# Decode of w_in in a PSUM bank, and the next chunk's transposes between the two halves of the second layer

## The chip, the cores and the metric

One core of a Trainium2 chip runs the kernel as one program. It has five engines with instruction queues of their own: TensorE (PE in the profile; its weight loads are PEld), VectorE (DVE), ScalarE (ACT), GpSimd (POOL) and SyncE (SP), which here only issues DMAs. The metric is the device time of one execution in microseconds (us).

## The reference

Attention, then a mixture of experts with a skip gate, then a two-layer net; everything in float32:

```
x   = attention(q, k, v)                  # block-causal, 4 x 8 heads, 576 tokens, head 64 -> x is 2304 x 512
do  = x @ w_skip > 0;  e = argmax(x @ w_gate)                # 8 experts
x[do] += gate * (relu(x @ w1[e]) @ w2[e])                    # w1: 512 x 1024, w2: 1024 x 512 per expert
h   = x @ w_in                                               # w_in: 512 x 2048
out = (max(h, 0) + alpha * min(h, 0)) @ w_out                # w_out: 2048 x 512
```

`w_in` and `w_out` come in as 64-bit floats, two 32-bit words per number, `hw` and `lw`; the kernel turns them into a float32 and splits that into two parts `hi` and `lo` for the matmuls. This turning is the "decode".

## The kernel before, in words

Three stages follow each other: attention (0 to about 265 us of the span), the experts (about 265 to 472 us) and the two-layer net (the rest). The change lies in the expert stage.

**Chunks of an expert.** For each expert `e` the list of its tokens is known. The first 32 go through a small path that packs tokens of four experts (`s_one`, `s_ht`, `s_two`). If there are more than 32 (a branch on the register `areg[e]`, in `extra`), the rest goes in chunks of 128 tokens. A chunk is gathered from the DRAM tensor `xd` by an indirect DMA that GpSimd issues (`gather`, line 579), transposed on TensorE through PSUM (`xt`, which calls `trans`, line 677; ScalarE copies the result to `xT`), goes through the first layer (`full1`, line 742: 32 matmuls, two ps_h tiles, ScalarE relu), and the second (`full2`, line 751: 8 matmuls of 512 columns, accumulated in one ps_y tile). ScalarE scales the result (line 753), GpSimd adds the old rows (line 754) and scatters the sum back to `xd` (line 582). The trace records each of these float32 matmuls twice, so full1 shows as x64 and full2 as x16. A last chunk of at most 64 tokens goes through `half` (lines 765 and 773).

`chunk` sets the order. On GpSimd the gather of the next chunk is issued before this chunk's add and scatter, so it stands behind the chunk before this one's add and scatter. On TensorE the next chunk's transposes stand between full1 and full2:

```
            if nxt:
                nxt.gather()
            ch.full1()
            if nxt:
                nxt.xt()
            ch.full2()
```

The first chunk of expert e+2 is gathered ahead (`level0`, after expert e is done). Where an expert has at most 32 tokens, its branch is skipped, and GpSimd then waits at the end of the skipped part until all its earlier DMAs have landed.

**Decode on VectorE.** w_in is 16 pieces of 128 x 512, decoded in the expert stage by `dec_in` (`decode` with `alone` and `halves`): ten VectorE operations (lines 628 to 636, 615 and 619) on each of two halves of 256 columns, with a scratch tile `dt` in SBUF for each half. `DEC` says how many pieces stand at which expert: none before and one behind the loads for expert 0's iteration, then 2 and 1, 2 and 2, 2 and 3, 3 and 0. The pieces of w_out and their decode (128 x 512 in one part, `w_dec`) come at the end of the stage (the first two, in `first_decode`) and in the first part of the last stage.

**Loads on SP.** All large loads stand in one queue, in program order, and a load waits until the one two places ahead has landed (`bulk`, DEPTH 2). A decode of piece m is followed by the load of piece m+3 (`dec_load`), which has to wait until VectorE has read piece m, since there are three raw tiles `dr`. Behind the loads of pieces 16, 17 and 18 (the first of w_out) stand the eight loads of expert 7's weights (`load_w(7)`), which also need that expert 4 is done with its buffers. Behind those, in `first_window`, stand the four loads of `xz`, the first 512 rows of x for the last stage; these wait for every gather and scatter before them. `first_window` also issues `s_two(7)` and the transposes of xz and the rows of the small path into four PSUM tiles `px` (lines 885 and 888), with which the last stage starts.

PSUM in the expert stage is eight banks: ps_t 2, ps_h 4, ps_y 2.

Of the kernel before, what the change touches and what calls it, by code (L numbers as in the profile page):

```python
# [9 lines left out]
F32 = mybir.dt.float32  # L10
# [7 lines left out]
PSUM = bass.MemoryType.PSUM  # L18
# [29 lines left out]
def tile_kernel(ctx: ExitStack, tc: tile.TileContext, q, k, v, w_skip, w_gate, w1, w2, w_in, w_out, alpha, out):  # L48
# [18 lines left out]
    wide = w_in.dtype != F32  # L67
# [529 lines left out]
    wpool["b2"] = mp("wb", 1)  # L597
    mw = mp("mw", 2)
    ps_t = mp("ps_t", 2, space=PSUM)
    ps_h = mp("ps_h", 4, space=PSUM)  # L600
    ps_y = mp("ps_y", 2, space=PSUM)

    def decode(n, hi, lo, tmp, alone, halves):
        wsp[n] = hi, lo
        a = raw.pop(n)
        V, P = nc.vector, nc.gpsimd
        parts = 2 if halves else 1
        n1 = 512 // parts
        cs = [slice(i * n1, i * n1 + n1) for i in range(parts)]
        ts = [tmp() if wide else a[:, c] for c in cs]  # L610

        def split():
            for t, c in zip(ts, cs):
                if halves:
                    V.tensor_copy(out=hi[:, c], in_=t)
                else:
                    nc.scalar.activation(out=hi[:, c], in_=t, func=AF.Copy)
            for t, c in zip(ts, cs):
                V.tensor_tensor(out=lo[:, c], in0=t, in1=hi[:, c].bitcast(F32), op=ALU.subtract)

        def each(fn):
            for t, c in zip(ts, cs):
                fn(t, t.bitcast(I32), a[:, c, 1], a[:, c, 0])

        if wide:
            if not alone:
                each(lambda t, ti, hw, lw: nc.scalar.activation(out=lw.bitcast(F32), in_=lw.bitcast(U32), func=AF.Copy, scale=2.0 ** -52))
            each(lambda t, ti, hw, lw: V.tensor_scalar(out=ti, in0=hw, scalar1=0x7FFFFFFF, scalar2=None, op0=ALU.bitwise_and))  # L628
            each(lambda t, ti, hw, lw: V.tensor_scalar(out=hw, in0=hw, scalar1=-2 ** 31, scalar2=None, op0=ALU.bitwise_and))
            each(lambda t, ti, hw, lw: V.tensor_scalar(out=t, in0=t, scalar1=_f32(TINY), scalar2=_f32(HUGE), op0=ALU.max, op1=ALU.min))  # L630
            each(lambda t, ti, hw, lw: V.tensor_scalar(out=ti, in0=ti, scalar1=4, scalar2=-2 ** 31, op0=ALU.logical_shift_left, op1=ALU.bitwise_xor))
            each(lambda t, ti, hw, lw: V.scalar_tensor_tensor(out=ti, in0=ti, scalar=1, in1=hw, op0=ALU.logical_shift_right, op1=ALU.bitwise_or))
            each(lambda t, ti, hw, lw: V.tensor_scalar(out=hw, in0=ti, scalar1=-2 ** 23, scalar2=None, op0=ALU.bitwise_and))
            if alone:
                each(lambda t, ti, hw, lw: V.scalar_tensor_tensor(out=lw.bitcast(F32), in0=lw.bitcast(U32), scalar=2.0 ** -52, in1=hw.bitcast(F32), op0=ALU.mult, op1=ALU.mult))
                each(lambda t, ti, hw, lw: V.tensor_tensor(out=t, in0=t, in1=lw.bitcast(F32), op=ALU.add))
            else:
                each(lambda t, ti, hw, lw: P.tensor_tensor(out=lw.bitcast(F32), in0=lw.bitcast(F32), in1=hw.bitcast(F32), op=ALU.mult))
                each(lambda t, ti, hw, lw: P.tensor_tensor(out=t, in0=t, in1=lw.bitcast(F32), op=ALU.add))
        if halves:  # L640
            split()
        return split
# [3 lines left out]
    def dec_in(n):  # L646
        for i in range(n):
            m = next(decs, None)
            if m is None:
                return  # L650
            hi = wip.tile([128, 512], F32R, tag="hi", name="whi")
            lo = wip.tile([128, 512], F32R, tag="lo", name="wlo")
            decode(m, hi, lo, lambda: mw.tile([128, 256], F32, tag="dt", name="dt"), True, True)
            if m + 3 < 19:
                dec_load(m + 3)

# [66 lines left out]
    class Chunk:  # L723
# [20 lines left out]
                nc.scalar.activation(out=h, in_=ps, func=AF.Relu)  # L744
                self.hT.append(h)

        def full2(self):
            w = wt[self.e][1]
            ps = ps_y.tile([128, 512], F32, tag="y", name="psy")
            for kk in range(8):  # L750
                nc.tensor.matmul(ps, self.hT[kk // 4][:, kk % 4], w[:, kk], start=(kk == 0), stop=(kk == 7))  # L751
            yo = mw.tile([128, DM], F32, tag="yo", name="yo")
            nc.scalar.activation(out=yo, in_=ps, func=AF.Copy, scale=self.gate)
            nc.gpsimd.tensor_tensor(out=yo, in0=yo, in1=self.xg, op=ALU.add)
            scatter(yo, self.ids)
# [33 lines left out]
    def chunk(e, ch, i, xg, xT):  # L789
        off = 32 + 128 * i  # L790
        nxt = Chunk(e, li[i + 1][:, e], xg[i % 2], xT[(i + 1) % 2]) if i + 1 < KX else None
        with tc.If(areg[e] > off + 64) as many:
            if nxt:
                nxt.gather()
            ch.full1()
            if nxt:
                nxt.xt()
            ch.full2()
            with tc.If(areg[e] > off + 128):
                if nxt:  # L800
                    chunk(e, nxt, i + 1, xg, xT)
                else:
                    with tc.For_i(off + 128, areg[e], 128) as r:
                        l = mw.tile([128, 2], I32, tag="ll", name="ll", bufs=1)
                        nc.gpsimd.dma_start(out=l, in_=lv[e, bass.ds(r, 128), :])
                        more = Chunk(e, l, xg[0], xT[0])
                        more.gather()
                        more.xt()
                        more.full1()
                        more.full2()  # L810
        with many.Else():
            ch.half()
# [4 lines left out]
    nxt = {}  # L817
# [56 lines left out]
    def first_window():  # L874
        xz = xzs[0]
        for t in range(4):
            nc.sync.dma_start(out=xz[:, t], in_=xd[t * 128:t * 128 + 128, :])
        for f in range(EARLY):
            dec_load(16 + f + 3)
        s_two(E - 1)  # L880
        new_x(0)
        px = [ps_h.tile([128, 4, 128], F32, tag="h", name="psx") for t in range(4)]
        for t in range(4):
            for kk in range(4):
                nc.tensor.matmul(px[t][:, kk], xz[:, t, kk * 128:kk * 128 + 128], ident, start=(kk == 0), stop=False, is_transpose=True, skip_group_check=True)
        for t in range(4):
            for kk in range(4):
                nc.tensor.matmul(px[t][:, kk], sy[1][:, kk * 128:kk * 128 + 128], xz[:, 5, t * 128:t * 128 + 128], start=False, stop=True, skip_group_check=True)
            split_x(0, t, px[t])
        for f in range(EARLY):  # L890
            w_split(f)
        for f in range(EARLY, 3):
            w_dec(f, lambda: xz[:, (6, 7, 4)[f]])
# [160 lines left out]
```

## Time and profile before

| what | value |
|---|---|
| three runs | 896.58, 897.37, 899.27 us; median 897.37 |
| profiled execution, its own time | 903.32 us |
| its span, first to last instruction | 901.7 us |
| TensorE busy | 818.0 us (91%) |
| VectorE busy | 440.4 us (49%) |
| GpSimd busy | 218.5 us (24%) |
| granted TensorE clock, mean | 0.952 of full speed |

The span is told in us from its start. The profiled execution took 0.66% longer than the median run; differences that are worked out in the span are taken off both. Busy shares are means over stages that differ: in the last stage (575 to 901.7 us) TensorE works 322.50 of 326.70 us, in the expert stage it waits in several places.

### The profile page before, as it was taken

To read this page: it belongs to the slowest core of one execution; us is meant where nothing else is said; L and a number is where in the kernel's file an instruction comes from. 1 tells how busy PE (TensorE), PEld (TensorE's weight loads), DVE (VectorE), ACT (ScalarE), POOL (GpSimd) and SP (SyncE) were. 2 spreads that over 40 slices of the span, in tenths; PEclk is the share of its full clock that TensorE was granted. 3 is DMA by queue.
4 is the path that set the end of the run, shared out by engine and by line. 5 is a ranking of instruction groups with operands and counts; after the bars stand their busy time and mean duration, and the time that the engine had idled before them with its cause. 6 is when DMAs were issued, how large, how long until landed. Compare 5 with 4: busy or idle time off the path is not lost.

```text
span 901.7 us, 15294 instructions
## 1 busy us (share of the span) xinstructions
PE 818.0 (91%) x5804; PEld 629.7 (70%) x5804; DVE 440.4 (49%) x1091; ACT 303.3 (34%) x793; POOL 218.5 (24%) x225
## 2 busy tenths in 40 slices
PE   7999999999975578857869988799999999999998
PEld 4777777777754454645547766588888888888897
DVE  4466757566646077654047999522332233223232
ACT  3666676766642121201225344321112111211121
POOL 1000110100126132243313654422222222222221
PEclk7999999999998698978979999899999999999999
DMA  6665354454215877762452222110011000100000
GB/s 132 150 181 138 79 140 104 113 128 134 74 51 123 260 249 246 227 221 84 141 188 91 79 74 67 47 47 1 0 48 47 1 1 23 47 1 1 23 26 24
DMA packets 96381, 85.87 MB, mean 95 GB/s; under 512 B 68601, under 2 KB 73913, under 8 KB 96272
## 3 DMA queue, kind: packets, MB, share of 16 engines
q1 hardware_dynamic: 93776, 78.88, 30.0%
q0 software_dynamic: 2496, 5.61, 2.2%
q8 instruction: 60, 0.98, 0.5%
q14 instruction: 49, 0.40, 0.1%
HBM read 73.20 MB, written 11.71 MB: 94 GB/s over the span
## 4 chain that ended last, share of the span: by engine, by line
PE 64%; DVE 11%; DMA 9%; issue 9%; POOL 3%; ACT 1%; another core or an unknown queue 1%; SPq 1%; POOLq 0%; DVEq 0%; ACTq 0%
PE psf L955 18%; PE psa L988 6%; PE psa L987 6%; PE pso L315 6%; PE psa L997 5%; PE pspt L296 5%; PE pss L236 5%; DMA xgs<-xd,sid 4%; PE psy L751 2%; PE pss L242 2%; PE pso L308 2%; DVE gt L966 2%; DVE mx L249 1%; DMA w1t<-in_moe_w_dram 1%; DVE dt L628 1%
## 5 line engine op out<-in xcount | busy, mean ns | idle before, releaser
L955 PE MATMUL psf<-xs,whi 128*128 128x512 f32 (+1 forms) x640 | 161.5, 375 | 6.1 <-ACT xs L843 6.1
L973 POOL TENSOR_TENSOR gl<-gt,gh 128x512 fp32r<-128x512 f32 (+1 forms) x72 | 85.3, 1185 | 250.4 <-PE psa L997 137.0
L955 PEld LDWEIGHTS psf<-xs,whi 128*128 128x128 f32 x640 | 115.5, 190 | 31.5 <-ACT xs L843 6.7
L972 ACT ACTIVATE gh<-gt 128x512 fp32r<-128x512 f32 (+1 forms) x80 | 47.1, 589 | 256.9 <-PE psa L988 149.7
L968 DVE TENSOR_SCALAR gu<-psf,alf 128x512 f32<-128x512 f32 (+1 forms) x64 | 43.7, 683 | 167.1 <-PE psf L955 166.9
L955 PE MATMUL psf<-xs,wlo 128*128 128x512 f32 (+1 forms) x320 | 81.0, 375 | 0.0
L266 ACT ACTIVATE pe<-pss,mx 128x512 f32<-128x512 f32 (+3 forms) x128 | 66.4, 522 | 12.0 <-DVE mx L249 10.1
L249 DVE TENSOR_REDUCE mx<-pss 128x2 f32<-128x1024 f32 (+1 forms) x64 | 52.5, 820 | 32.2 <-PE pss L238 29.3
L955 PEld LDWEIGHTS psf<-xs,wlo 128*128 128x128 f32 x320 | 57.2, 190 | 11.8
L274 ACT ACTIVATE pt<-pspt 128x512 f32<-128x512 f32 (+3 forms) x112 | 52.0, 487 | 34.9 <-PE pspt L296 33.5
L987 PE MATMUL psa<-whi,gh 128*128 128x512 f32 x144 | 57.6, 400 | 4.0 <-ACT gh L972 4.0
L315 PE MATMUL pso<-pt,vr 128*64 128x128 f32 x640 | 59.7, 285 | 0.6 <-ACT pt L274 0.5
L987 PE MATMUL psa<-wkg,gh 128*128 128x512 f32 x144 | 56.8, 395 | 1.5 <-ACT gh L972 1.5
L988 PE MATMUL psa<-wlo,gh 128*128 128x512 f32 x144 | 56.4, 392 | 0.0
L988 PE MATMUL psa<-wkg,gh 128*128 128x512 f32 x144 | 56.3, 391 | 0.0
L628 DVE TENSOR_SCALAR dt<-dr 128x256 int32<-128x256 int32 (+1 forms) x45 | 24.1, 567 | 60.4 <-DMA dr<-in_moe_w_in_dram 56.0
L296 PE MATMUL pspt<-ident,pe 128*128 128x128 f32 x320 | 52.9, 289 | 0.0
L315 PEld LDWEIGHTS pso<-pt,vr 128*64 128x64 f32 x640 | 39.2, 136 | 9.5 <-issue 3.1
L969 DVE SCALAR_TENSOR_TENSOR gt<-psf,gu 128x512 f32<-128x512 f32 (+1 forms) x64 | 40.0, 625 | 10.7 <-POOL gl L973 4.6
L677 PE MATMUL pst<-ident,xg 128*128 128x128 f32 x32 | 7.3, 357 | 38.7 <-DMA xg<-xd,li 35.9
L296 PEld LDWEIGHTS pspt<-ident,pe 128*128 128x128 f32 x320 | 34.4, 141 | 11.2 <-issue 9.6
L742 PEld LDWEIGHTS psh<-xT,w1t 128*128 128x128 f32 x320 | 39.6, 206 | 1.7 <-issue 1.0
(237 smaller groups left out, 1486.1 us busy)
## 6 DMA issues: line engine op xcount, KB each, us to landing
w1t<-in_moe_w_dram SPq DMA_DIRECT2D x32, 512.0 KB, 4.9
w2t<-in_moe_w_dram SPq DMA_DIRECT2D x32, 512.0 KB, 4.5
dr<-in_moe_w_in_dram SPq DMA_DIRECT2D x16, 512.0 KB, 4.7
dr<-in_moe_w_out_dram SPq DMA_DIRECT2D x16, 512.0 KB, 3.6
out_dram<-ob SPq DMA_DIRECT2D x18, 256.0 KB, 2.0
qr<-in_q_dram SPq DMA_DIRECT2D x32, 128.0 KB, 4.6
kr<-in_k_dram SPq DMA_DIRECT2D x32, 128.0 KB, 2.6
vr<-in_v_dram SPq DMA_DIRECT2D x32, 128.0 KB, 2.5
```

Source lines behind the costliest of these rows:

```text
L236: nc.tensor.matmul(ps[:, x, 0:n], d[a][hs, qc], d[b][hs, 0:n], start=(k == 0), stop=False)
L249: nc.vector.tensor_reduce(out=m, in_=ps[:, :, 0:128 * i + 128], axis=AX.X, op=ALU.max, negate=True)
L266: ins = nc.scalar.activation(out=pt[:, x, 0:n], in_=ps[:, x, 0:n], func=AF.Exp, bias=m[:, x:x + 1], scale=1.0, accum_out=d["sum"][:, x * 4 ...
L274: nc.scalar.activation(out=o, in_=a, func=AF.Copy)
L296: nc.tensor.transpose(ps[:, y, j, :], e[:, x, j * 128:j * 128 + 128], ident)
L315: nc.tensor.matmul(d["o"][hs, i * 128:i * 128 + 128], v5[:, j, x, :], d["pt", i][:, x, j, :], start=(j == 0), stop=(j == i))
L955: nc.tensor.matmul(ps[:, 0:n], wsp[f // 4 * 4 + kk][a][:, ws], c[:, kk, 0:n], start=(n0 == 0 and kk == 0), stop=(n0 == 2 and kk == 3))
L972: nc.scalar.activation(out=hi[:, 0:n], in_=t[:, 0:n], func=AF.Copy)
L973: (nc.gpsimd if w or f % 2 else nc.vector).tensor_tensor(out=lo[:, 0:n], in0=t[:, 0:n], in1=hi[:, 0:n].bitcast(F32), op=ALU.subtract)
L987: nc.tensor.matmul(o, hi[:, ts], whi, start=(f == 0), stop=False)
L988: nc.tensor.matmul(o, hi[:, ts], wlo, start=False, stop=False)
L997: nc.tensor.matmul(acc[w, t], lo[:, t * 128:t * 128 + 128], whi, start=False, stop=False)
```

## The change

The scratch tile of the w_in decode becomes one whole PSUM bank (a new pool ps_d, for which ps_h gives one of its four), and the decode works on 512 columns at once, so each piece takes ten VectorE instructions where there were twenty. In `full2` the next chunk's transposes stand between the fourth and the fifth of the eight matmuls. One of the four px tiles lies in the new bank. Line numbers behind it move by one or two.

```diff
-    ps_h = mp("ps_h", 4, space=PSUM)
+    ps_h = mp("ps_h", 3, space=PSUM)
     ps_y = mp("ps_y", 2, space=PSUM)
+    ps_d = mp("ps_d", 1, space=PSUM)
...
-        parts = 2 if halves else 1
-        n1 = 512 // parts
-        cs = [slice(i * n1, i * n1 + n1) for i in range(parts)]
-        ts = [tmp() if wide else a[:, c] for c in cs]
+        cs = [slice(0, 512)]
+        ts = [tmp() if wide else a]
...
-            decode(m, hi, lo, lambda: mw.tile([128, 256], F32, tag="dt", name="dt"), True, True)
+            decode(m, hi, lo, lambda: ps_d.tile([128, 512], F32, tag="d", name="dt"), True, True)
...
-        def full2(self):
+        def full2(self, nxt=None):
...
             for kk in range(8):
+                if nxt and kk == 4:
+                    nxt.xt()
                 nc.tensor.matmul(ps, self.hT[kk // 4][:, kk % 4], w[:, kk], start=(kk == 0), stop=(kk == 7))
...
-            if nxt:
-                nxt.xt()
-            ch.full2()
+            ch.full2(nxt)
...
-        px = [ps_h.tile([128, 4, 128], F32, tag="h", name="psx") for t in range(4)]
+        px = [ps_h.tile([128, 4, 128], F32, tag="h", name="psx") for t in range(3)]
+        px.append(ps_d.tile([128, 4, 128], F32, tag="d", name="psx"))
```

TensorE, at the start of an expert with more than 32 tokens (xg: the gathered chunk, xT: the transposed one, hT: the first layer's output); first before, then after the change:

```order
L782 COMPARE_AND_BRANCH
L677 MATMUL pst<-ident,xg 128x128 x4
L792 COMPARE_AND_BRANCH
L742 MATMUL psh<-xT,w1t 128x128 x32
L677 MATMUL pst<-ident,xg 128x128 x4
L751 MATMUL psy<-w2t,hT 128x512 x8
L799 COMPARE_AND_BRANCH
```

```order
L783 COMPARE_AND_BRANCH
L676 MATMUL pst<-ident,xg 128x128 x4
L793 COMPARE_AND_BRANCH
L741 MATMUL psh<-xT,w1t 128x128 x32
L752 MATMUL psy<-w2t,hT 128x512 x4
L676 MATMUL pst<-ident,xg 128x128 x4
L752 MATMUL psy<-w2t,hT 128x512 x4
L798 COMPARE_AND_BRANCH
```

The four transposes moved behind half of the second layer; nothing was added on TensorE.

VectorE, the decode of one piece of w_in (dr: the raw words, dt: the scratch tile, whi and wlo: the two parts); first before, then after the change:

```order
L628 TENSOR_SCALAR dt<-dr 128x256 x2
L629 TENSOR_SCALAR dr<-dr 128x256 x2
L630 TENSOR_SCALAR dt<-dt 128x256 x2
L631 TENSOR_SCALAR dt<-dt 128x256 x2
L632 SCALAR_TENSOR_TENSOR dt<-dt,dr 128x256 x2
L633 TENSOR_SCALAR dr<-dt 128x256 x2
L635 SCALAR_TENSOR_TENSOR dr<-dr 128x256 x2
L636 TENSOR_TENSOR dt<-dt,dr 128x256 x2
L615 CAST whi<-dt 128x256 x2
L619 TENSOR_TENSOR wlo<-dt,whi 128x256 x2
```

```order
L627 TENSOR_SCALAR dt<-dr 128x512
L628 TENSOR_SCALAR dr<-dr 128x512
L629 TENSOR_SCALAR dt<-dt 128x512
L630 TENSOR_SCALAR dt<-dt 128x512
L631 SCALAR_TENSOR_TENSOR dt<-dt,dr 128x512
L632 TENSOR_SCALAR dr<-dt 128x512
L634 SCALAR_TENSOR_TENSOR dr<-dr 128x512
L635 TENSOR_TENSOR dt<-dt,dr 128x512
L614 CAST whi<-dt 128x512
L618 TENSOR_TENSOR wlo<-dt,whi 128x512
```

The ten steps are the same; eight of them now read or write dt in PSUM, and the two on dr alone (L628 and L634 after the change) stay in SBUF.

## Rows read from the trace of the kernel before

**Rows 1.** Timeline of TensorE: start us, us, instructions, [idle before <- releaser].
```profile
302.45 1.09 PE L677 MATMUL pst<-ident,xg 128*128 128x128 f32 x4 [14.35 <-DMA xg<-xd,li]
...
340.16 1.09 PE L677 MATMUL pst<-ident,xg 128*128 128x128 f32 x4 [5.34 <-DMA xg<-xd,li]
...
375.71 7.03 PE L751 MATMUL psy<-w2t,hT 128*128 128x512 f32 x16
...
398.98 1.09 PE L677 MATMUL pst<-ident,xg 128*128 128x128 f32 x4 [9.09 <-DMA xg<-xd,li]
...
421.38 1.09 PE L677 MATMUL pst<-ident,xg 128*128 128x128 f32 x4 [5.98 <-DMA xg<-xd,li]
```

**Rows 2.** GpSimd: all gathers of chunks (ns min/median/max), and its timeline.
```profile
L579 POOL DMA_INDIRECT xg<-xd,li x13: 945/974/10022, 278.3 to 454.3; - x13
DMA to landing us min/median/max: 3.4/6.1/13.1
...
278.32 10.02 POOL L579 DMA_INDIRECT xg<-xd,li  x1 [4.92 <-DMA li<-lst]
...
329.70 3.73 POOL L579 DMA_INDIRECT xg<-xd,li  x1 [0.56 <-POOL pad L65]
...
383.60 7.64 POOL L754 TENSOR_TENSOR yo<-yo,xg 128x512 f32<-128x512 f32 x1 [11.54 <-ACT yo L753]
...
409.12 6.96 POOL L754 TENSOR_TENSOR yo<-yo,xg 128x512 f32<-128x512 f32 x1 [15.31 <-ACT yo L753]
...
432.26 1.27 POOL L754 TENSOR_TENSOR yo<-yo,xg 128x512 f32<-128x512 f32 x1 [13.61 <-ACT yo L753]
```

**Rows 3.** VectorE timeline: start of the last three decodes, and last steps of two runs.
```profile
286.72 0.77 DVE L619 TENSOR_TENSOR wlo<-dt,whi 128x256 fp32r<-128x256 f32 x2
...
399.54 0.49 DVE L628 TENSOR_SCALAR dt<-dr 128x256 int32<-128x256 int32 x2 [9.43 <-DMA dr<-in_moe_w_in_dram]
...
414.18 0.78 DVE L619 TENSOR_TENSOR wlo<-dt,whi 128x256 fp32r<-128x256 f32 x2
```

**Rows 4.** Groups by shape, VectorE: operation, shapes, count | busy us, mean ns | idle before.
```profile
L276 DVE COPY xt<-pso 128x512 f32<-128x512 f32 x16 | 10.9, 682 | 1.3 <-PE pso L315 1.3
```

**Rows 5.** Timeline of VectorE, then of GpSimd, 563 to 567 us.
```profile
563.98 0.68 DVE L844 TENSOR_TENSOR xs<-psx,xs 128x512 fp32r<-128x512 f32 x1
...
565.43 1.52 DVE L628 TENSOR_SCALAR dt<-dr 128x512 int32<-128x512 int32 x1
...
563.60 1.37 POOL L638 TENSOR_TENSOR dr<-dr 128x512 f32<-128x512 f32 x1 [3.48 <-issue]
565.04 1.62 POOL L639 TENSOR_TENSOR dt<-dt,dr 128x512 f32<-128x512 f32 x1
```

**Rows 6.** VectorE timeline of a decode in one part of 512 columns, all in SBUF.
```profile
452.92 0.69 DVE L632 SCALAR_TENSOR_TENSOR xz<-xz,dr 128x512 int32<-128x512 int32 x1
453.65 0.43 DVE L633 TENSOR_SCALAR dr<-xz 128x512 int32<-128x512 int32 x1
```

**Rows 7.** SP timeline at the end of the expert stage, and SP's waits.
```profile
403.69 10.55 SPq L79 DMA_DIRECT2D dr<-in_moe_w_out_dram  x3
437.91 6.42 SPq L79 DMA_DIRECT2D w1t<-in_moe_w_dram  x4
446.42 8.76 SPq L79 DMA_DIRECT2D w2t<-in_moe_w_dram  x4
464.26 3.42 SPq L877 DMA_DIRECT2D xz<-xd  x4
...
SPq L79 <- PE psy L773: 23.6, 1, 23.6
...
SPq L877 <- DMA xd<-yo,sid: 8.1, 1, 8.1
```

**Rows 8.** TensorE timeline, start of the matmuls that fill px.
```profile
466.67 1.95 PE L709 MATMUL psy<-w2t,hts 128*32 128x128 f32 x64 [1.29 <-ACTq L782]
...
471.60 3.74 PE L888 MATMUL psx<-xz,ys 128*128 128x128 f32 x32
```

## The prediction, written before the changed kernel was run

> **What bounds the kernel now.** I read the busy times by stage first. The last stage works TensorE without a gap and the attention is not touched, so the change can only move the start of the last stage, the matmuls that fill px at 471.60 us [rows 8]. What happens before them is read from three timelines.
>
> TensorE's timeline shows where the expert stage loses time: it stands before the transposes of a gathered chunk [rows 1]. The wait at 302.45 (14.35 us) is for expert 2's first chunk; those at 340.16 (5.34), 398.98 (9.09) and 421.38 (5.98) are for a next chunk, whose transposes the change moves. A smaller one of 1.14 at 375.24 makes 35.9 us in all. The full2 behind it took 7.03 us.
>
> GpSimd's timeline says why the gathers are late [rows 2]. A gather takes it 0.97 us at the median and an add 1.27, yet one gather took 10.02, one 3.73, and two adds 7.64 and 6.96. Set beside VectorE [rows 3]: its first three decodes end at 286.72 + 0.77 = 287.49, and the 10.02 us gather ends at 288.34, one gather's work later. The last three decodes end at 414.96, and the add of 409.12 ends at 416.08, again one add's work later. So GpSimd got nothing done until the run of decodes was over. The other two long instructions end within 1.2 us of the end of a run of decodes as well.
>
> SP's timeline says what else must be done by then [rows 7]. The loads of pieces 16 to 18 end at 414.24, expert 7's weights are issued from 437.91 on, after 23.6 us of waiting for expert 4's last matmuls, and xz at 464.26, after 8.1 us of waiting for the last GpSimd DMAs.
>
> **The decode gets slower.** Of the ten steps nine get one instruction of 512 columns that either has a tensor in PSUM or two tensor inputs; the tenth (hw on itself) stays a one-input step in SBUF. A one-input step of 512 columns within SBUF takes 0.43 us and the two-input step 0.69, and a step that needs the one before starts 0.04 us after its end (452.92 to 453.65) [rows 6]. A one-input copy out of PSUM takes 0.68 [rows 4], as much as a two-input step. No row has VectorE write to PSUM. The bounds for these steps are 0.43 (as in SBUF) and 0.75, and since the nearest row with PSUM on one side is the copy, I take 0.69 for all nine. That is 9 x 0.73 + 0.46 = 7.0 us a piece; with all steps at 0.60 it is 5.9, at 0.86 it is 8.2. Before, pieces followed each other every 5.1 us (399.54 to the end at 414.96 are three). So 16 pieces cost VectorE some 30 us more. The Trainium skill (VectorE: DVE Perf Modes, "Why PSUM operands drop a tier") says that a float32 step with any PSUM operand runs at one element a cycle, which speaks against this change. By that rule the piece costs the same 7.0 us; the row of the copy agrees.
>
> Most of it is hidden: VectorE waits between the runs of decodes for the bulk loads (9.43 us before 399.54 [rows 3]), and a run of three takes 21 us in place of 15. Only the last run has somebody waiting. Piece 18's load needs the eighth step of the last of the three: 399.54 + 2 x 7.0 + 5.6 = 419.1, where its issue ended the burst at 414.24. The extra gathers among the bulk loads may make piece 13 land up to 4 us later; I take 1. So expert 7's loads can start at about 420.5, if expert 4 is done.
>
> **GpSimd is let free.** A row of the last stage shows the kind of operation that does and that doesn't get in the way: while GpSimd worked from 563.60 to 564.97, a VectorE step with an input from PSUM took its plain 0.68, but a one-input step within SBUF, normally 0.43, took 1.52 while GpSimd worked from 565.04 on [rows 5]. After the change only two of ten steps are all in SBUF (0.43 and 0.69 of 7.0 us). So I let every GpSimd instruction take its plain time plus nothing; bound from above: 1.1 us each.
>
> Then, in the trace's times: the first gather is issued at 278.32 as before but done at 279.3, the next at 280.7, so that the branches of the skipped experts, which wait for landings, let expert 2's gather go 9 us earlier. Its transposes come at 293.4 instead of 302.45 (-9.1), and all of expert 2 and the start of expert 3 with them. The 3.73 us gather loses 2.8; its chunk would be landed at about 328.4 (6.3 us from issue to landing, as there).
>
> **The transposes.** Half of full2 is 3.5 us [rows 1]. Expert 3's full1 ends at about 325.9, half of full2 at 329.4, so nothing is left of 5.34, and TensorE, which ran full2 in 8.79 us behind that wait (9.14 was the longest in the trace), runs it in 7.03: another -7.1, together -16. Expert 4: 1.14 goes. Its next add takes 1.3 instead of 7.64, so the gather lands by 375.6, while full1 ends at 372.9 and the half at 376.4; all of 9.09 goes, and the 5.98 of the chunk behind it in the same way, each with 1 to 2 us of the slower full2. Expert 4 would be done at 403.5 instead of 439.5: 36 us of which 12 need the new place of the transposes at most.
>
> **But TensorE is then early for nothing.** Expert 7's loads start at 420.5, not at 403. From their first issue to their last took 437.91 to 455.18 = 17.3 us, and xz was ready to go 1.0 us later (464.26 less the 8.1 of waiting) [rows 7]; GpSimd is through by 428, so that wait is gone. xz is issued at 438.8 instead of 464.26. From there to the matmuls at 471.60 took 7.3 us [rows 8]: 446.1. The other way: w2 of expert 7 lands some 5 us after its last issue, at 442.8; s_two(7) starts then, and from its start to 471.60 there were 4.93 us, with some room: 447.1. I take 447.1, a gain of 24.5 us. Everything behind keeps its order and its pace: window 0 of the last stage decodes in SBUF as before.
>
> ps_h with three banks in place of four costs nothing: a chunk uses two, whose readers (0.6 us each on ScalarE) are done a whole layer before their turn comes again. If that cover were gone it would be 0.6 us a chunk. The px tile in ps_d waits for the last decode, at 421, far ahead of 447.
>
> 903.3 - 24.5 = 878.8 for the profiled execution. The median of the runs is 897.4; 24.5 off gives **872.9 us**.
>
> **Rivals.**
>
> *The load chain gives more.* If a piece takes 5.1 us in PSUM too, expert 7's loads start at 414.3 and xz goes at 432.6; TensorE's side then binds: about -30, 867 us. Against it: the copy out of PSUM at 0.68.
>
> *GpSimd stays locked out.* If any dense run of VectorE steps keeps it out, not just those in SBUF, then the last add waits for the last decode: 399.54 + 21 = 420.5 instead of 415.0, 5.5 us later, and the second half of full2, 3.5 to 4.5 us, is all that is won back. Expert 4 ends about 1 us later than before: 898. With 8.2 us a piece it is 4.5 us later: 902. It turns to a loss above 6.7 us a piece. For it: steps with two inputs, which are slow in SBUF anyway, did not let GpSimd in during these runs either. Against it: rows 5. The Trainium skill (SBUF — State Buffer, "Who interferes with whom") says that whoever starts first gets the shared pair of ports for one instruction, and the other waits for that one. By that rule a wait of 10 us over twenty and more instructions would not come from the ports; the sum would be that of this rival, 898. The trace disagrees with its plain reading: four GpSimd instructions ended just behind a run.
>
> *Only part of it.* If GpSimd's adds are still held up by the two steps in SBUF and the gathers take longer among the bulk loads, expert 4 ends 15 to 25 us early instead of 36 and the branches behind it take their time: 10 to 18 us gained, 880 to 887.
>
> *The change does not do it.* The written order has both moves in it, so this is only the case in which the start of the last stage is held by something that I don't see: within 2.7 us of before.
>
> **How the numbers follow.** The forecast (-20 to -29 us) 0.74; more 0.07; part of it 0.10; GpSimd locked out 0.07 (0.05 slower, 0.02 the same); no effect 0.02. Differences under 0.3% (2.7 us) can't be told from none here. Faster 0.91, same 0.04, slower 0.05. The forecast's own range is 868 to 878 from 5.9 to 8.2 us a piece and 0 to 4 us on the bulk loads. With the case above and the part case it is 864 to 885.
>
> **What would show it right or wrong.** No chunk gather or add on GpSimd above 2.1 us; the wait before expert 2's transposes at about 5 us; no wait, or under 2 us, before the other transposes, which stand between two groups of eight full2 records; decode steps in PSUM at 0.69 and runs of three at 21 us; SP no longer waiting for expert 4 but for VectorE before expert 7's loads; and TensorE with a new wait of some 10 us for expert 7's weights. Wrong it would be if the long GpSimd instructions are still there, or if a step that writes to PSUM takes 1 us and more.

## The result, and the profile after

| | before | after |
|---|---|---|
| median of the runs, same chip | 896.98 us (895.14 to 899.27, 4 runs) | 876.21 us (874.04 to 877.65, 4 runs) |
| ratio, 95% interval | | 0.9759 (0.9732 to 0.9785) |
| profiled execution: own time, span | 903.32, 901.7 us | 874.04, 872.4 us |
| mean granted TensorE clock | 0.952 | 0.968 |

The change makes the kernel 2.4% faster, 20.8 us by the medians; 872.9 us was forecast. The two traces differ by more, 29.3 us, since the profiled execution of before lies above its median and that of after below. Where experiments give a ratio, it is to executions of the kernel before on their own chip; in each series these fell into two groups, 894 to 904 and 909 to 916 us, and the ratios use the first group alone.

TensorE's timeline after, with the places that answer to [rows 1] and [rows 8] (columns as there; xt is now line 676, full2 line 752, the px matmuls line 888, and 692 is the first layer of the small path, here expert 7's):

```profile
297.45 0.38 PE L676 MATMUL pst<-ident,xg 128*128 128x128 f32 x2
...
374.67 3.60 PE L752 MATMUL psy<-w2t,hT 128*128 128x512 f32 x8
378.11 0.60 PE L676 MATMUL pst<-ident,xg 128*128 128x128 f32 x4
378.55 3.60 PE L752 MATMUL psy<-w2t,hT 128*128 128x512 f32 x8
...
419.46 1.08 PE L692 MATMUL psh<-w1t,xts 128*32 128x256 f32 x8 [4.80 <-DMA w1t<-in_moe_w_dram]
423.99 2.31 PE L692 MATMUL psh<-w1t,xts 128*32 128x256 f32 x16 [3.45 <-DMA w1t<-in_moe_w_dram]
428.59 1.08 PE L692 MATMUL psh<-w1t,xts 128*32 128x256 f32 x8 [2.29 <-DMA w1t<-in_moe_w_dram]
...
443.25 4.02 PE L888 MATMUL psx<-xz,ys 128*128 128x128 f32 x32
```

No transposes wait for a gather any more; the row of 378.11, between two halves of full2 without a bracket, is like those at 310.00, 332.25, 363.66 and 392.56. Instead TensorE waits 10.5 us for expert 7's weights. The px matmuls start at 443.25 in place of 471.60 [rows 8]: 28.3 of the 29.3 us lie ahead of them. Of these 1.5 lie ahead of the expert stage's first gather, that of the small path's rows (264.49 before, 262.97 after), and 26.8 between it and the px matmuls.

GpSimd's timeline after, for [rows 2]:

```profile
276.12 0.98 POOL L579 DMA_INDIRECT xg<-xd,li  x1 [4.30 <-DMA li<-lst]
...
368.55 1.83 POOL L755 TENSOR_TENSOR yo<-yo,xg 128x512 f32<-128x512 f32 x1 [9.94 <-ACT yo L754]
...
397.45 1.28 POOL L755 TENSOR_TENSOR yo<-yo,xg 128x512 f32<-128x512 f32 x1 [10.61 <-ACT yo L754]
```

Its chunk gathers and its adds as groups (count, ns min/median/max, first and last start):

```profile
L579 POOL DMA_INDIRECT xg<-xd,li x13: 944/974/1232, 276.1 to 417.2; - x13
...
L755 POOL TENSOR_TENSOR yo<-yo,xg x5: 1263/1277/1836, 315.0 to 397.5; 128x512 f32<-128x512 f32 x5
```

The gather that took 10.02 us takes 0.98, and no add takes over 1.84. VectorE's timeline beside that last add shows the two kinds of step (for [rows 4] to [rows 6]; the first row starts the last run of three decodes, the last one ends it):

```profile
394.02 0.69 DVE L627 TENSOR_SCALAR dt<-dr 128x512 int32<-128x512 int32 x1 [1.88 <-DMA dr<-in_moe_w_in_dram]
...
397.29 0.69 DVE L632 TENSOR_SCALAR dr<-dt 128x512 int32<-128x512 int32 x1
398.02 1.26 DVE L634 SCALAR_TENSOR_TENSOR dr<-dr 128x512 f32<-128x512 uint32 x1
399.31 0.70 DVE L635 TENSOR_TENSOR dt<-dt,dr 128x512 f32<-128x512 f32 x1
...
414.58 0.69 DVE L618 TENSOR_TENSOR wlo<-dt,whi 128x512 fp32r<-128x512 f32 x1
```

While the add runs from 397.45 to 398.73, the step with its input in PSUM (line 632) takes its plain 0.69; the step that lies in SBUF alone (line 634) ends only 0.55 after the add. The add, which starts inside the step of line 632 (397.29 to 397.98), takes its plain 1.28, so it waited neither for the end of that step nor for a gap. The step with a tensor in PSUM and GpSimd go on side by side; the step all in SBUF and GpSimd take turns.

SP's timeline after, for [rows 7]:

```profile
400.04 14.14 SPq L79 DMA_DIRECT2D dr<-in_moe_w_out_dram  x3
414.27 10.03 SPq L79 DMA_DIRECT2D w1t<-in_moe_w_dram  x4
425.24 7.45 SPq L79 DMA_DIRECT2D w2t<-in_moe_w_dram  x4
437.01 1.76 SPq L876 DMA_DIRECT2D xz<-xd  x4
```

And the wait of SP that stands longest there (us in all, times, longest):

```profile
SPq L79 <- DVE dr L632: 19.4, 4, 12.9
```

The wait of 23.6 us for expert 4's matmuls is gone. Its place is taken by one of 12.9 us in which the load of a w_out piece waits until VectorE has read the raw tile, with expert 7's weights queued behind it.

### The profile page after: what moved, and what is told of

It is laid out like the page before. It is cut to its first block, busy times and chain, and to the rows that moved or that the text cites. A ratio compares the mean times of both kernels' runs of the same rounds, so it can differ in the third digit from the quotient of the medians.

```text
span 872.4 us, 15135 instructions
## 1 busy us (share of the span) xinstructions
PE 809.5 (93%) x5804; PEld 622.0 (71%) x5804; DVE 460.5 (53%) x931; ACT 302.8 (35%) x793; POOL 195.2 (22%) x225
## 4 chain that ended last, share of the span: by engine, by line
PE 37%; DVE 12%; DMA 9%; issue 3%; ACT 1%; POOL 1%; SPq 0%; DVEq 0%; ACTq 0%; POOLq 0%
PE psf L955 18%; PE psa L988 6%; PE psa L987 6%; PE psa L997 6%; DMA w1t<-in_moe_w_dram 3%; DMA w2t<-in_moe_w_dram 3%; DVE dt L627 2%; DVE gt L966 2%; DMA dr<-in_moe_w_in_dram 2%; DVE dr L628 1%; DVE dt L631 1%; DVE dt L630 1%; DMA dr<-in_moe_w_out_dram 1%; DVE dt L629 1%; DVE wlo L618 1%
## 5 line engine op out<-in xcount | busy, mean ns | idle before, releaser
L249 DVE TENSOR_REDUCE mx<-pss 128x2 f32<-128x1024 f32 (+1 forms) x64 | 52.5, 820 | 31.2 <-PE pss L238 29.3
L843 DVE TENSOR_TENSOR xs<-psx,xs 128x512 fp32r<-128x512 f32 x18 | 12.4, 690 | 56.9 <-ACT xs L842 56.9
L627 DVE TENSOR_SCALAR dt<-dr 128x512 int32<-128x512 int32 x29 | 24.3, 838 | 33.2 <-DMA dr<-in_moe_w_in_dram 28.9
L692 PE MATMUL psh<-w1t,xts 128*32 128x256 f32 x256 | 21.1, 473 | 22.0 <-DMA w1t<-in_moe_w_dram 10.5
```

The source lines that it names most:

```text
L249: nc.vector.tensor_reduce(out=m, in_=ps[:, :, 0:128 * i + 128], axis=AX.X, op=ALU.max, negate=True)
```

## The experiments

The main theory was the prediction's: the decode in PSUM lets GpSimd go on (M), the gathers and adds come early, and what binds next is the chain of loads behind the last run of decodes. Rivals: it is not the memory but VectorE's instructions, their number and length (C, W) or their order (D), or the gain comes from the new place of the transposes. The last column is the time in the trace from the expert stage's first gather (of the small path's rows) to the px matmuls:

| run | ratio to before | 95% interval | series | expert stage, us |
|---|---|---|---|---|
| kernel before, first and second trace | 1 | | | 207.1, 207.3 |
| changed kernel, at the result | 0.9759 | 0.9732 to 0.9785 | | 180.3 |
| decode alone | 0.9830 | 0.9796 to 0.9863 | 1 | 185.4 |
| transposes alone | 0.9974 | 0.9954 to 0.9995 | 1 | 202.1 |
| SBUF, one part of 512 | 0.9791 | 0.9751 to 0.9830 | 1 | 182.2 |
| expert 7's loads first | 0.9699 | 0.9665 to 0.9733 | 1 | 174.1 |
| SBUF, halves in turn | 0.9822 | 0.9798 to 0.9845 | 2 | 184.8 |
| PSUM, halves alternating | 0.9815 | 0.9789 to 0.9841 | 2 | 187.5 |
| new decode for the last six pieces | 0.9802 | 0.9767 to 0.9837 | 2 | 186.3 |
| SBUF, two gaps a piece | 0.9740 | 0.9687 to 0.9793 | 3 | 177.7 |
| changed kernel again | 0.9795 | 0.9746 to 0.9844 | 3 | 180.9 |
| loads first, SBUF 512 | 0.9727 | 0.9691 to 0.9762 | 3 | 176.8 |

In these traces 263.0 to 267.6 us pass ahead of that first gather and 429.2 to 432.4 behind the start of the px matmuls, in no order that goes with the kernel. Ratios whose intervals overlap are not clearly apart.

**The decode alone.** The changed kernel with the transposes back ahead of full2:

```
-            ch.full2(nxt)
+            if nxt:
+                nxt.xt()
+            ch.full2()
```

> The changed kernel with the transposes back in front of full2; the decode stays in the PSUM bank. Theory A (GpSimd is let free by the decode in PSUM; expert 7's loads behind the last decodes then set the end): TensorE waits 2 to 3 us again before each of four groups of transposes, 10 to 11 us in all, which is about as much as it was early for expert 7's loads, so the time stays within 3 us of the changed kernel: 876 to 879 us. Theory B (the new place of the transposes brings most of the gain): 886 us and more.

Measured: 882.92 us, between the two times given. GpSimd is free (chunk gathers and adds of 128 rows at or under 1.32 us), so the larger share of the gain is the decode's. TensorE's waits for gathers are back (us in all, times, longest):

```profile
PE pst L676 <- DMA xg<-xd,li: 10.0, 4, 3.4
```

The timeline where it loses to the changed kernel, GpSimd and then SP:

```profile
435.69 0.95 POOL L579 DMA_INDIRECT xg<-xd,li  x1 [0.76 <-POOL pad L65]
...
420.93 7.79 SPq L79 DMA_DIRECT2D w1t<-in_moe_w_dram  x4
...
446.28 2.00 SPq L878 DMA_DIRECT2D xz<-xd  x4
```

The four waits, 10.0 us, push expert 4's end to 422.6, and behind it stand the gathers of experts 6 and 7, the last at 435.69 (417.21 in the changed kernel); xz goes 7.9 us after the last load of w2 has been issued. This execution reached the expert stage 4.2 us later than the changed one; within the stage it took 185.4 us against 180.3 and 180.9. So the new place is worth some 5 us in the traces (by the ratios 6, or 3 against the changed kernel's second series, whose interval overlaps), which the slack that I had counted on does not swallow.

**The transposes alone.** The kernel before, with `full2(nxt)` as in the change and the old decode:

> The kernel before with only the transposes moved into the middle of full2; the decode stays in SBUF in two halves, ps_h keeps four banks. Theory A: GpSimd is still locked out until each run of decodes ends, and those ends are set by the loads; only the last half of full2 is won at the end of expert 4: 4 to 5 us, 892 us, with two adds of 7 us and a gather of 10 us still there. Theory B: the four waits shrink by 3.5 us each, 11 us and more, 886 us or less.

Measured: 895.23 us, 0.26% faster, less than either theory gave, with the long instructions still there. GpSimd's two longest adds, and VectorE's last step ahead of the end of the second:

```profile
378.97 10.61 POOL L756 TENSOR_TENSOR yo<-yo,xg 128x512 f32<-128x512 f32 x1 [10.46 <-ACT yo L755]
404.35 10.26 POOL L756 TENSOR_TENSOR yo<-yo,xg 128x512 f32<-128x512 f32 x1 [12.20 <-ACT yo L755]
...
412.73 0.76 DVE L619 TENSOR_TENSOR wlo<-dt,whi 128x256 fp32r<-128x256 f32 x2
```

The add of 404.35 ends at 414.61, 1.1 us after the run of decodes (413.49). The later place of the transposes gives little while the gathers and the adds ahead of them are shut out; together the two edits give 2.4%, one by one 1.7% and 0.3%.

**The work tile back in SBUF, in one part.** The changed kernel but for

```
-            decode(m, hi, lo, lambda: ps_d.tile([128, 512], F32, tag="d", name="dt"), True, True)
+            decode(m, hi, lo, lambda: mw.tile([128, 512], F32, tag="dt", name="dt", bufs=1), True, True)
```

> The changed kernel with the scratch tile of the decode in SBUF, one part of 512 columns, ten instructions a piece; the transposes in the middle of full2, ps_h three banks. Theory A: a piece takes about 5.4 us, GpSimd is locked out as before, 891 to 894 us. Theory C (it is the number and length of the instructions that lets GpSimd in, not the memory): long GpSimd instructions gone and 871 to 876 us, since the decode is faster than in PSUM.

Measured: 878.67 us, above theory C's 876 and far from A's 891. GpSimd is as free as in the changed kernel, with no tensor in PSUM: gathers up to 1.35 us, adds of 128 rows up to 1.50. The add of 397.78 and the VectorE step beside it:

```profile
397.78 1.45 POOL L755 TENSOR_TENSOR yo<-yo,xg 128x512 f32<-128x512 f32 x1 [10.20 <-ACT yo L754]
...
398.13 1.39 DVE L632 TENSOR_SCALAR dr<-dt 128x512 int32<-128x512 int32 x1
```

Here the two take turns by one instruction: the step waits for the add and not the add for the run. So PSUM is not needed for the gain. The kernel before had shown it in a row that I passed over: a gather among the SBUF decodes of 512 columns [rows 6] took 1.31 us.

```profile
454.32 1.31 POOL L579 DMA_INDIRECT xg<-xd,li  x1 [0.77 <-POOL pad L65]
```

**Halves in turn, halves alternating.** The change had done two things to the decode: another memory, and one chain of 512-column steps in place of two halves that alternate. Two runs part them further: SBUF with ten steps on one half and then ten on the other (each needs the one before it), and PSUM with the old alternation.

```
-        cs = [slice(0, 512)]
+        n1 = 256 if halves else 512
+        cs = [slice(i, i + n1) for i in range(0, 512, n1)]
...
+            for t, c in zip(ts, cs):
+                one(hi, lo, a, t, c)
```

(`one` does the ten steps on one half; the PSUM run has the first three lines alone, with both halves in one ps_d tile.)

> The changed kernel with the decode's work tile back in SBUF as two halves of 256 columns, as before the change, but the ten steps of one half run first and then the ten of the other, so that each instruction needs the result of the one just before it; before the change the two halves alternated, and every second instruction was independent of its neighbour. Theory D (the memory is of no account; GpSimd gets in wherever VectorE's next instruction has to wait for the one before it, and is shut out where independent instructions stand back to back): gathers and adds of GpSimd under 2 us, no wait of TensorE for a gather, time 876 to 881. Theory W (256-column instructions in SBUF, twice as many, are what shuts it out; 512 columns a step let it in): gathers and adds of 4 to 10 us come back, time 893 to 900, as when the transposes alone were moved (895.2).

> The changed kernel with its decode still in the PSUM bank, but as two halves of 256 columns whose steps alternate, in the order that the kernel before had. Theory D (back-to-back independent instructions shut GpSimd out, wherever their tile lies): long GpSimd gathers and adds come back, 4 to 10 us each, time 893 to 900. Theory M (that of the prediction: a step with a tensor in PSUM doesn't shut GpSimd out): they stay under 2 us, time 874 to 879; then either of the two, PSUM or a dependent chain, is enough by itself.

Measured: 884.79 and 885.59 us where the kernel before took 901.32, by the ratios 881 and 880 where it takes 897; that is 4 to 5 us above the changed kernel, which was not run on that chip. The traces show it in the expert stage (184.8 and 187.5 us against 180.3 and 180.9): the pieces take 7.1 us (two halves of 3.56) and 7.7 in place of 6.9, and TensorE waits 20.4 and 19.3 us for expert 7's weights in place of 10.5 and 12.9; why the loads ahead of the last run of decodes come later as well is open, and so are waits of 3.7 and 7.8 us for gathers, where D and M had none. In both GpSimd is free: the adds, min/median/max, first with the halves in turn, then in PSUM:

```profile
L774 POOL TENSOR_TENSOR yo<-yo,xg x5: 1268/1331/1372, 313.2 to 396.1; 128x512 f32<-128x512 f32 x5
...
L757 POOL TENSOR_TENSOR yo<-yo,xg x5: 1265/1269/1272, 312.1 to 394.2; 128x512 f32<-128x512 f32 x5
```

Neither the width nor the number of the instructions shuts it out (W falls): the run with the halves in turn has the same twenty instructions in the same memory as the run with the transposes alone, in another order. What sets before apart is in the last column of VectorE's groups, its idle time just ahead of such a step; the next three fences are of 262 to 425 us. Before:

```profile
L615 DVE CAST whi<-dt 128x256 fp32r<-128x256 f32 x32 | 7.9, 293 | 0.0
L631 DVE TENSOR_SCALAR dt<-dt 128x256 int32<-128x256 int32 x32 | 7.8, 289 | 0.0
```

SBUF, halves in turn:

```profile
L610 DVE TENSOR_SCALAR dt<-dt 128x256 int32<-128x256 int32 x32 | 11.7, 365 | 1.1
L615 DVE CAST whi<-dt 128x256 fp32r<-128x256 f32 x31 | 10.3, 331 | 1.1
```

PSUM, halves alternating:

```profile
L632 DVE TENSOR_SCALAR dt<-dt 128x256 int32<-128x256 int32 x32 | 13.8, 432 | 1.1
L616 DVE CAST whi<-dt 128x256 fp32r<-128x256 f32 x32 | 12.1, 419 | 0.6
```

A dependent step starts 0.03 us after the one before it (1.1 us over 32). In the kernel before, the alternating halves in SBUF overlap, the next instruction starting some 0.08 us before the end of the last, and VectorE is empty only between runs; an add that starts at 320.90, in the gap of 0.32 us ahead of the step of 321.06, takes its plain 1.28. In PSUM even alternating halves leave 0.02 to 0.03. The gap is not what lets GpSimd in there, though: an add of the PSUM run starts inside a step, as the one of 397.45 in the changed kernel did, and takes its plain time.

```profile
394.17 1.27 POOL L757 TENSOR_TENSOR yo<-yo,xg 128x512 f32<-128x512 f32 x1 [10.51 <-ACT yo L756]
...
393.96 0.90 DVE L632 TENSOR_SCALAR dt<-dt 128x256 int32<-128x256 int32 x2
```

The first of the two steps ends at about 394.4; an add that waited for that would have taken 1.5. So D's "wherever their tile lies" falls, and M holds for steps with a tensor in PSUM.

**Two gaps a piece.** The alternating halves in SBUF as before the change, but for the last two of the ten steps:

```
                 if halves:
                     V.tensor_copy(out=hi[:, c], in_=t)
+                    V.tensor_tensor(out=lo[:, c], in0=t, in1=hi[:, c].bitcast(F32), op=ALU.subtract)
...
             for t, c in zip(ts, cs):
-                V.tensor_tensor(out=lo[:, c], in0=t, in1=hi[:, c].bitcast(F32), op=ALU.subtract)
+                if not halves:
+                    V.tensor_tensor(out=lo[:, c], in0=t, in1=hi[:, c].bitcast(F32), op=ALU.subtract)
```

> The changed kernel with the decode in SBUF as two alternating halves of 256 columns, as before the change, but for its last two steps (whi and wlo), which one half does in turn and then the other, so that two of the twenty instructions of a piece wait for the one just before them, at the piece's end. Theory D (GpSimd gets in at any moment at which no VectorE instruction is under way; the rows of the kernel before show none from the start of a run of decodes to its end): a GpSimd gather or add that starts within a piece waits for the end of that piece at the most, so none takes over 1.3 + 5.1 = 6.4 us and on average they take 2.5 us more than plain, where the kernel before and the run with the transposes alone had up to 10.6; time 880 to 888. If two gaps in twenty are too few to let it in: gathers and adds of 7 to 11 us as before, time 893 to 897.

Measured: 873.29 us, faster than the 880 to 888 expected, and than the changed kernel's 879.04 on the same chip (871.26 to 878.69 against 875.43 to 881.24). The longest of its adds of 128 rows and the VectorE steps around, with the gap:

```profile
373.23 2.95 POOL L758 TENSOR_TENSOR yo<-yo,xg 128x512 f32<-128x512 f32 x1 [10.41 <-ACT yo L757]
...
374.07 0.78 DVE L638 TENSOR_TENSOR dt<-dt,dr 128x256 f32<-128x256 f32 x2
374.74 0.31 DVE L615 CAST whi<-dt 128x256 fp32r<-128x256 f32 x1
375.09 1.38 DVE L616 TENSOR_TENSOR wlo<-dt,whi 128x256 fp32r<-128x256 f32 x1
```

The add stands from 373.23 on, through overlapping steps, to the first gap, 375.05 to 375.09. It ends at 376.18, a plain 1.26 later within 0.2, and the VectorE step behind the gap takes 1.38 in place of 0.43. The two other long ones of this run, a multiplication of 64 rows at 346.43 (4.30, plain 1.57) and the add of 402.78 (2.18), show the same, and the step behind their gap is stretched as well. For instructions in SBUF D is shown: one gap of 0.03 us is enough, and two a piece do for the time at least what PSUM does. The pieces take 5.4 us here in place of 6.9, expert 7's first load goes at 410.53 (416.92 in the changed kernel beside it), and no wait of TensorE for w1t is shown. Shorter pieces alone don't explain the better time: in the SBUF run of one part they take 5.6 us, yet that load goes at 413.96, TensorE waits 12.2 us for w1t, and the time is the changed kernel's.

**Expert 7's loads first.** The changed kernel with its last three decodes, and so the loads of pieces 16 to 18, behind those of expert 7's weights:

```
-DEC = ((0, 1), (2, 1), (2, 2), (2, 3), (3, 0), (0, 0), (0, 0), (0, 0))
+DEC = ((0, 1), (2, 1), (2, 2), (2, 3), (0, 3), (0, 0), (0, 0), (0, 0))
```

> The changed kernel with the eight loads of expert 7's weights put ahead of the decode of pieces 13 to 15 in program order, and so ahead of the loads of pieces 16 to 18 on SP. Theory A (the loads of expert 7 behind the last run of decodes set the end): they start at expert 4's end, some 10 us earlier, and the matmuls that fill px come 6 to 10 us earlier: 866 to 870 us. If something else sets the end: 875 to 878 us, or later, if the first pieces of w_out come too late for the last stage.

Measured: 871.31 us, the fastest of all, 1.3 us above what theory A gave. SP's timeline, and where px now waits:

```profile
401.58 7.10 SPq L79 DMA_DIRECT2D w1t<-in_moe_w_dram  x4
410.39 8.29 SPq L79 DMA_DIRECT2D w2t<-in_moe_w_dram  x4
420.99 5.16 SPq L79 DMA_DIRECT2D dr<-in_moe_w_out_dram  x3
431.48 1.79 SPq L876 DMA_DIRECT2D xz<-xd  x4
...
434.17 1.55 PE L885 MATMUL psx<-ident,xz 128*128 128x128 f32 x8 [4.26 <-DMA xz<-xd]
```

The weights go 12.7 us sooner, as expert 4's last matmuls (399.60 to 403.28) let go of its buffers. So the last run of decodes did hold them. That gives 4.9 us by the medians of two series and 6.2 in the expert stage of the traces, and not 12.7, since xz then has the loads of the w_out pieces ahead of it.

**New decode for the last six pieces only.** Pieces 0 to 9 decoded as before:

```
+        n1 = 256 if halves and n < 10 else 512
...
+            decode(m, hi, lo, lambda: mw.tile([128, 256], F32, tag="dt", name="dt") if m < 10 else ps_d.tile([128, 512], F32, tag="d", name="dt"), True, True)
```

> The changed kernel with the old decode (SBUF, alternating halves) for the first ten pieces and the new one, in PSUM, for the last six. By the prediction's account the end of expert 4 has slack against the loads of expert 7's weights (404.8 against 414.3 in the changed kernel), which themselves follow the last run of decodes. If that holds, a long first gather and a long gather or two among the first ten pieces cost expert 2 and 3 their 9 to 15 us but the end only what goes beyond 9.5 us: 876 to 882. If every microsecond that GpSimd gains counts, the time lies in the middle between the two kernels, 884 to 890.

Measured: 883.48 us, in one series with the two runs of halves (884.79, 885.59), in which GpSimd was free throughout. The long gather is back, with its wait on TensorE:

```profile
282.05 9.38 POOL L579 DMA_INDIRECT xg<-xd,li  x1 [5.58 <-PE psy L709]
...
304.69 1.09 PE L677 MATMUL pst<-ident,xg 128*128 128x128 f32 x4 [12.95 <-DMA xg<-xd,li]
```

Even so TensorE still waits for expert 7's weights at the end (10.2 us). Its waits for gathers come to 16.4 us in this run, where the changed kernel has none, and the expert stage takes 186.3 us, 5.4 to 6.0 more than the changed kernel's. So some 10 us of the 16.4 are swallowed by the slack ahead of expert 7's weights, about the 9.5 given, and the rest reaches the end. The time itself was above the 882 given, on a chip where the kernel before took 4 us more; by the ratio it is 879 where that takes 897.

**Both kernels again, and two edits together.** The kernel before once more, the changed one once more, and the loads first with the SBUF tile of 512.

> The kernel before, unchanged, for a second trace: its first trace was of an execution 6 us above the median of its runs. If the extra 6 us lie in the expert stage, the long gathers and adds will be shorter or fewer here and the px matmuls start at 464 to 468 in place of 471.6; if they lie in the stage of attention or the last stage, those stages will be shorter and the distance from the first gather to the px matmuls the same 207 us.

> The changed kernel as it is, beside the other runs on the same chip, for a second trace of it and a time that can be set against theirs: 876 us where the kernel before takes 897, or the same ratio of 0.976 where the chip is another. If the executions on the chip of the last runs, where the kernel before took 901, were slower for all kernels alike, nothing in the trace of this one but the bulk loads should move by more than 1 to 2 us.

> Expert 7's loads ahead of the last three decodes, and the decode's work tile in SBUF in one part of 512 columns (pieces of 5.2 us in place of 6.9). If the chain of bulk loads alone sets the end once they go first, the decode's own length is of no account: 869 to 873, the same as the run with the loads first (871.3). If the last three decodes were still on the path through the loads of the w_out pieces: 866 to 869.

Measured: the kernel before 902.29 us (one run), the changed one 879.04, the last 872.42. The second trace of before has other long instructions (a gather of 7.57 us at 280.26, adds of 4.22, 3.92, 4.49 and 6.01) and the same end:

```profile
407.73 6.01 POOL L754 TENSOR_TENSOR yo<-yo,xg 128x512 f32<-128x512 f32 x1 [14.38 <-ACT yo L753]
...
471.26 3.84 PE L888 MATMUL psx<-xz,ys 128*128 128x128 f32 x32
```

Its px matmuls start 207.3 us after the stage's first gather (263.99), as in the first trace. But this execution was as long as the first, and so were the parts ahead of and behind the expert stage; neither of the two cases expected came, and two traces of 902 and 903 us can't show what sets the median of 897 apart. An estimate can: with the shortest time ahead of the stage in any trace (262.97), the shortest behind px (429.20) and the 1.6 us by which an execution's own time exceeds its span, 896.98 leaves at most 203.2 us for the expert stage. So a good part of the 6 us lies in that stage after all, and the traces show more gain than the medians. With the second trace of after (px at 444.92, on another chip) the gain ahead of px is 26.3 us, and 23.6 by the traces' own times; in the expert stage the two pairs of traces agree, 26.8 and 26.4. With the loads first, shorter pieces bring nothing, as the first of the two cases has it: 872.42 against 871.31, on two chips.

## Why the prediction was right, step by step

The time (872.9 forecast, 876.21 measured), the sign and the chain of causes held, but a step of it named too narrow a reason, and the closeness of the time is in part luck.

- **The decode gets slower: right.** 7.0 us a piece was forecast from the copy out of PSUM [rows 4]; the start of one piece to the next is 6.90, and the last run of three takes 394.02 to 415.27, 21.25 where 21 was forecast (one step in it stretched by an add). Steps that write to PSUM take 0.69 to 0.70 like those that read it.
- **GpSimd is let free: right in what happens, too narrow in why.** Plain times plus nothing were forecast, 1.1 us more as the bound; the worst add is 0.57 above plain. That a step with a tensor in PSUM doesn't get in GpSimd's way is shown by the rows of after. What failed is the sentence that set "any dense run of VectorE steps" against "just those in SBUF". The lock-out of before took both SBUF and independent instructions without a gap; a chain in SBUF lets GpSimd in as well. Where the halves still alternate in SBUF without a gap the rival's lock-out is there: the transposes alone, 895.23 us. The rule of the Trainium skill that the prediction weighed (SBUF — State Buffer, "Who interferes with whom": who issues first holds the shared pair for that one instruction) agrees with the run in SBUF of one part, where each side waits for one instruction. It doesn't tell what before shows (10.02 us [rows 2]): where the next instruction was under way 0.08 us before the last had ended, GpSimd got nothing until the run was over. Here the measurement decides.
- **The transposes: the waits vanish, as forecast.** But expert 2's began at 297.45, not at 293.4. The wait for its gather is gone, where 5 us were forecast; TensorE itself came later. Its small path started at 273.43 after 5.05 us of waiting for ScalarE's first copy of xts, which wasn't there in before; it shows in the traces of some kernels with and without the change, and what makes it is open. Expert 4 ends at 404.78 where 403.5 was forecast. That the place of the transposes accounts for 12 us of waits "at most" was right (10.0 in the run without it), but they were not all within the slack: some 5 us of them reach the end, through the gathers of experts 6 and 7 behind expert 4.
- **TensorE is early for nothing: right.** A wait of 10 us for expert 7's weights was forecast, 10.5 measured, and the run with the loads first shows that the last decodes held them. Its size was off: the loads start at 414.27, not 420.5. The run of decodes itself began at 394.02 in place of 399.54, behind bulk loads that went earlier (389.07 in place of 393.59), where I had put them 1 us later. Of that some came back: xz goes 4.3 us after the last issue of w2, not 1.0. The sum at xz is 437.01 against 438.8, and px starts at 443.25 against 447.1 (the second way of the prediction adds up to 442.8 + 4.93 = 447.7; the 0.6 taken off it has no row); 1.5 us of that lies ahead of the expert stage, whose first gather is at 262.97 in place of 264.49.
- **ps_h with three banks: nothing seen.** No wait of TensorE for a reader of ps_h stands in the expert stage.

The forecast's 24.5 us lie between the gain of the medians (20.8) and that of the first pair of traces (29.3), near the second pair's 23.6. They were worked out in a trace 6 us longer than the median and taken off the median as they stood. In the traces' expert stage the gain was 26.8 and 26.4, so the sum itself was some 2 us short; the step to the median took the stage of a median execution to be as long as the trace's, which by the estimate above it is not, and so gave up to 6 us too much. The two errors have opposite signs, and what is left, 3.3 us, is no more than executions of one kernel differ (4.1 us before, 3.6 after).

## What to carry to other kernels

On VectorE and GpSimd here, a run of independent VectorE instructions in SBUF shut GpSimd out to the end of the run; look in the profile for long instructions of the one engine that end just behind a run of the other, and for an idle column of 0.0 in that run. Two dependent pairs in a piece of 5.4 us were enough to end it, and cost less than the move to another memory (pieces of 6.9 us). After a wait is removed, look for the next thing in the same queue: here it was the place of eight loads behind three decodes, a change of two numbers worth 4.9 us.

## What the runs showed of the hardware that was not expected

- GpSimd gets in at a gap of 0.03 us between two VectorE instructions: three of three long instructions of the run with two gaps a piece ended one plain instruction after the first such gap (within 0.2 us), while without gaps one took 10.02 us in place of 0.97.
- Two independent VectorE instructions of 256 columns overlap by 0.08 us where they write to SBUF (the kernel before), and leave 0.03 us between them where they write to PSUM (0.43 us each, the second 0.47 after the first, in the run of alternating halves in PSUM).
- While GpSimd adds, a VectorE step with a tensor in PSUM keeps its 0.69 us, and one in SBUF alone goes from 0.69 to 1.26. GpSimd needs no gap beside a step with a tensor in PSUM: adds that started inside such a step took their plain 1.28 and 1.27 us.
